# Fewer row maxima behind mid-product visits, a fixed score tile, another bank and a longer wait for blocks in a fused attention and MLP kernel

## The chip, the cores and the metric

The kernel runs on one core of one Trainium2 chip. The core has a matrix engine (PE, with its weight loads listed apart as PEld), a vector engine (DVE), a scalar engine (ACT), GpSimd (POOL), a sync engine (SP) that issues most transfers, and 16 DMA engines. Matrix products land in PSUM, whose banks hold 128 x 512 float32 values each; DVE and ACT read them from there. The metric is the device time of one execution in microseconds (us); lower is better.

## The reference

One transformer block with conditioning: a layer norm with scale and shift, softmax attention with 16 heads of width 28 over 2048 tokens of width 448, a gated residual, a second layer norm with scale and shift, an MLP of width 1792, and a second gated residual.

```python
mod = (_silu(c) @ w_mod).reshape(c.shape[0], 6, 1, -1)
sa, ca, ga, sb, cb, gb = (mod[:, 0], ..., mod[:, 5])
h = _layernorm(x, axis=-1) * (1 + ca) + sa
x = x + ga * _A_ref(h, A_wqkv, A_wo)      # softmax(q k^T / sqrt(28)) v, then wo
h = _layernorm(x, axis=-1) * (1 + cb) + sb
x = x + gb * _B_ref(h, B_w1, B_b1, B_w2, B_b2)   # layernorm, w1, gelu, w2
```

Softmax is taken with the maximum of each row subtracted. The maximum has to be known before the exponentials, so the kernel computes rough scores a second time for the maxima alone.

## The kernel before

Heads are taken in four groups `g` of four heads `j`. The 28 rows of head `j` lie on partitions 32`j` to 32`j`+27, so a product over 28 rows uses one of four row groups of the matrix engine. Queries come in four blocks `qt` of 512; a **unit** `u = 4g + qt` is one group and one block of queries. Keys come in four blocks `cch` of 512, or in 16 tiles `kt` of 128.

**A row maximum** (`max_one`, L478) is one product of 128 queries with 512 keys of one head into one PSUM bank (`max_mm`, L476) and a DVE reduction of that bank (L481). A full problem has 1024 of them. Some are taken in pairs: `pair_diff` (L485) and `open_pair` (L630) multiply with the difference of two key blocks, let ACT take the positive part (L489, L641), and a second product with one DVE operation (L493, L648) adds it and reduces. A pair costs two products and one DVE operation in place of two. Differences of key blocks are made on POOL by `make_kd` (L603). The banks for maxima go round in `mx_ring` (`ps_mx`): `ma`, `ma`, `m2`, `m2`, `m1` in the projection stage, later `m1`, `m2`, `m2` or `m1` alone. When a bank's turn comes, the product waits until DVE or ACT has read it.

**The projection stage** (to about 170 us) goes block by block of 512 tokens, `b` = 0 to 3, through a list of tasks `n`: chains of 11 products for q, k (`qk_task`, L396 by way of `mm_acc`) and v (`v_task`). After each chain `emit_task` (L687) puts a few maxima, four for `b` = 0 and five after it, one more where `sixth` holds: first the difference products, then single maxima with the second products of the pairs set in at place two. For the tasks (1,1), (1,3), (1,5), (1,7) and (2,8), `emit_mid` (L715) puts up to four more maxima between the halves of the chain. These are the mid-product visits. The tasks (1,0) to (1,3) end with products for the modulation rows (`mod_mm`, L747).

**The attention stage** (about 170 to 818 us) has 256 steps, 16 for each unit. A step computes two score tiles of 128 keys by 1024 (two heads each, three products for the split of float32 into a high and a low part: 12 products, L1297), lets ACT take exponentials of each tile (L1310, two for a step) and puts the products with v of the step before (L1255) behind them. Maxima are set in between. Up to step 118 a step works with two score tiles `s1`, `s0` and three or four maxima (`open_pair` on odd steps). From step `RING` = 119 on there is a ring of three score tiles: `third_tile` takes the two `m2` banks for `s2`, the first score tile is `s0`, the second `s1` or `s2` in turn, and the third of them serves for one wide pair of maxima (`emit_pair`, one DVE reduction of 1024 values, L684); a single maximum uses `m1`. That is three maxima a step. In steps 8 to 11 of the last four units (`is_wo`) the ring is left: `t_wo` (L1030) puts chains for the output projection into a bank of `mx_ring`, ACT copies the result (L1044), and `m2` serves maxima again. When all maxima are done, `three` is set and the ring goes on with score tiles alone.

Blocks of queries and keys of the next group are loaded by `load_hi` (L508) when the blocks before them are done with; `loaded` notes the step from which they may be used, three steps on. `emit_single` and `emit_pair` choose among `ready_max()`. `max_fin` and its `put` (L528) write a unit's negated maxima into its query tile some steps before the unit begins.

**The MLP stage** (to the end) runs chains of 11 products (L396) and three products for each token tile (L1376 to L1378) back to back.

Of the kernel before, what the change touches and what calls it, by code (L numbers as in the profile page):

```python
# [33 lines left out]
LAST_MAX = NKT - 4  # L34
RING = 119
PAIR_AT = (2, 2, 0, 2)
# [8 lines left out]
def tile_adaln_block(ctx: ExitStack, tc: tile.TileContext, x, wqkv, wo, w1, b1, w2, b2, c, w_mod, out):  # L45
# [22 lines left out]
    mx_ring = ["ma", "ma", "m2", "m2", "m1"]  # L68
# [39 lines left out]
    def ps_mx():  # L108
        mx_ring.append(mx_ring.pop(0))
        return ps_tile(mx_ring[-1], 1 if mx_ring[-1] == "m1" else 2)  # L110
# [392 lines left out]
    def load_hi(kind, g, b):  # L503
        loaded[(kind, g, b)] = clock[0] + 3
        tg = ("kh" if kind else "qh") + str(b)
        t = sb.tile([128, 512], F32R, tag=tg, name=nm(tg), bufs=1)
        (kh_sb if kind else qh_sb)[(g, b)] = t
        sp.dma_start(f(t), f(dscr[kind][0][g])[:, b * 512 : (b + 1) * 512])  # L508
        if kind and b in (PAIR_AT[g], PAIR_AT[g] + 1) and all((g, PAIR_AT[g] + c) in kh_sb for c in range(2)):
            at(clock[0] + 4, lambda: make_kd(g))  # L510
# [91 lines left out]

    def make_kd(g):  # L603
        if g and any(m[0] == kd["g"] for m in pairable()):
            at(clock[0] + 2, lambda: make_kd(g))
            return
        c0 = PAIR_AT[g]
        kd.update(g=g, t=slot("d0h", [128, 1, 512]), **{"from": clock[0] + 1})
        pool.tensor_tensor(out=kd["t"][:, 0, :], in0=f(kh_sb[(g, c0 + 1)]), in1=f(kh_sb[(g, c0)]), op=ALU.subtract)
# [81 lines left out]
    def emit_task(n, sixth, n_pairs):  # L691
# [4 lines left out]
        js = [m[3] for m in pairs]  # L696
        n_ops = n - len(pairs) + (sixth and len(pairs) > 0)
        singles = []
        for x in range(n_ops - len(pairs)):
            if mxq:  # L700

                free = [j for j in range(4) if j not in js] or range(4)
                fits = [y for y, m in enumerate(mxq[:16]) if m[:3] == mxq[0][:3] and m[4] == free[x % len(free)]]
                singles.append(mxq.pop(fits[0] if fits else 0))
        ops = [lambda ps, m=m: max_one(*m, ps) for m in singles]
        ops[2:2] = rests
        for x, op in enumerate(ops):
# [7 lines left out]
    def emit_mid():  # L715
        for j in range(4):
            fits = [x for x, m in enumerate(mxq[:16]) if m[4] == j]
            if fits:
                m = mxq.pop(fits[0])
                max_one(*m)  # L720
                count(*m[:2], [m[2]])

    p1_n = [0, False, 1, None]

# [88 lines left out]
    for b in range(NB):  # L813
# [12 lines left out]
        for n, (tb, kind, g) in enumerate(tasks):  # L826
# [11 lines left out]
            p1_n[2] = (3 if n > 4 else 1) if b == 3 else 2 if b == 2 and p1_n[1] else 1  # L838
            p1_n[3] = emit_mid if (b, n) in ((1, 1), (1, 3), (1, 5), (1, 7), (2, 8)) else None
            if kind < 2:  # L840
                fn = qk_task(tb, kind, g, firsts[n] if b == 0 and n < 3 else None)
# [70 lines left out]
    for key in ("s0", "s1"):  # L912
        ps_open(key)
    turns = ("s1", "s2")

# [73 lines left out]
    def unit_end_tasks(u, o_sb):  # L989
# [40 lines left out]
        def t_wo(t):  # L1030
            def go():
                p = ps_mx()
                ts = slice(t * 128, (t + 1) * 128)
# [229 lines left out]
    for u in range(NU):  # L1263
        g, qt = divmod(u, NB)
        for kt in range(NKT):
# [7 lines left out]
            if not (three or mxq or late):  # L1273
                three = True
                s_ring[:] = ["s0", turns[step % 2], turns[1 - step % 2]]
            now[0] = turns[step % 2]
# [13 lines left out]
            for n, hf in enumerate((first, 1 - first)):  # L1290
                s2 = ps_s2() if three else ps_two((now[0] if n else "s0") if ring else ("s1", "s0")[n if step < RING else 1 - n])
                for term, (kp, qp) in enumerate(((0, 0), (1, 0), (0, 1))):
# [149 lines left out]
```

## Time and profile before

| | |
|---|---|
| median of 3 runs | 1115.26 us (1115.2 to 1115.96) |
| profiled execution, its own time | 1116.36 us |
| its span, first to last instruction | 1114.3 us |
| PE busy | 1101.0 us, 99% of the span |
| DVE, ACT, POOL busy | 806.9, 693.2, 214.7 us |
| granted PE clock | 1.000 |

Views of the profile are read as follows. A row of the timeline has the start in us from the begin of the span, the length in us, the engine and line of the kernel, the operation with output<-inputs (buffer numbers left out: `m` is a bank of maxima, `s` a score tile, `pa` a chain's bank), partitions x elements, and the count of merged instructions; in brackets stands the idle time before it and what ended it. Products on PE overlap: one takes about 0.4 to 0.5 us from start to end, while the next may start after 0.2 us, or at once on another row group. So the busy share of PE hides small stalls, and the distance from start to start is what has to be read. A row of stretches gives, for a stretch of the span, its length, the busy time of each engine with the count of instructions, the granted clock, the share of the DMA engines and their GB/s.

### The profile page before, as it was taken

Reading aid. Unit: us, or ns where it says so; the run is one execution under the profiler, and the core shown is the slowest. Engines: PE = TensorE matmul, PEld = TensorE weight load, DVE = VectorE, ACT = ScalarE, POOL = GpSimd, SP = SyncE. Lnnn points to the kernel's source line nnn. Section 1 sums busy time; section 2 is a strip of 40 time slices with the busy share of each in tenths; the row PEclk is TensorE's granted clock in tenths of the full one; section 3 lists DMA queues with packets and bytes.
Section 4 is the critical chain, followed back from the end, with each engine's and each line's share of the span. In section 5 each row is a group of like instructions: output and inputs, shape, how many; then the busy total and the mean of one; then the engine's idle time right before and its main releaser. Section 6 shows DMA issues by size and latency. Waiting matters only on the chain.

```text
span 1114.3 us, 20698 instructions
## 1 busy us (share of the span) xinstructions
PE 1101.0 (99%) x8319; PEld 667.1 (60%) x8319; DVE 806.9 (72%) x1392; ACT 693.2 (62%) x878; POOL 214.7 (19%) x215
## 2 busy tenths in 40 slices
PE   8999999999999999999999999999999999999998
PEld 5756675444444444444444454544568888888887
DVE  6969788999999999988888867584558844444322
ACT  4555667888888888888888878577752311111210
POOL 1633332110000000000100020206214514023000
PEclk9999999999999999999999999999999999999999
DMA  9553354221231211221211402112222100000000
GB/s 307 204 187 97 100 179 129 58 68 30 77 96 51 68 41 46 67 90 58 69 40 59 125 30 87 58 30 75 75 81 67 31 34 1 1 34 1 34 1 34
DMA packets 49341, 81.19 MB, mean 73 GB/s; under 512 B 12311, under 2 KB 18702, under 8 KB 49234
## 3 DMA queue, kind: packets, MB, share of 16 engines
q1 hardware_dynamic: 48762, 79.14, 22.8%
q8 instruction: 65, 1.06, 0.4%
q10 hardware_dynamic: 148, 0.46, 0.1%
q0 software_dynamic: 336, 0.28, 0.1%
q14 instruction: 30, 0.25, 0.1%
HBM read 55.04 MB, written 26.48 MB: 73 GB/s over the span
## 4 chain that ended last, share of the span: by engine, by line
PE 93%; DVE 3%; ACT 1%; DMA 1%; issue 1%; SPq 0%; POOL 0%; DVEq 0%; ACTq 0%; POOLq 0%
PE s L1297 22%; PE o L1255 22%; PE m L396 16%; PE pa L396 9%; PE m L476 8%; PE s L1377 3%; PE s L1376 3%; PE s L1378 3%; PE s L476 1%; DVE mxp L481 1%; PE t L1377 1%; PE t L1378 1%; PE t L1376 1%; PE ma L476 1%; DMA slot_c<-in_w_mod_dram 1%
## 5 line engine op out<-in xcount | busy, mean ns | idle before, releaser
L481 DVE TENSOR_REDUCE mxp<-m 128x1 f32<-128x512 f32 x564 | 366.0, 686 | 82.9 <-PE m L476 66.4
L1297 PE MATMUL s<-slot_b,slot_a 28*128 28x512 f32 (+1 forms) x3072 | 358.1, 424 | 0.5 <-ACT slot_c0h L1310 0.5
L1297 PEld LDWEIGHTS s<-slot_b,slot_a 28*128 28x128 f32 (+1 forms) x3072 | 211.2, 183 | 170.7 <-ACT slot_c L1310 93.1
L476 PE MATMUL m<-kh,qh 28*128 28x512 f32 x598 | 221.6, 470 | 1.8 <-DMA kh<-d 1.0
L1310 ACT ACTIVATE slot_c<-s 128x1024 f32<-128x1024 f32 x170 | 174.7, 1027 | 53.5 <-PE s L1297 52.7
L1255 PE MATMUL o<-slot_c,v 128*32 128x512 f32 x680 | 178.9, 605 | 0.0
L1353 ACT ACTIVATE full<-m,b_col 128x512 f32<-128x512 f32 x56 | 38.5, 688 | 191.9 <-PE m L396 179.7
L1255 PE MATMUL o<-slot_c1h,v 128*32 128x512 f32 x512 | 134.7, 605 | 0.9 <-ACT slot_c1h L1310 0.9
L1255 PE MATMUL o<-slot_c0h,v 128*32 128x512 f32 x512 | 134.7, 605 | 0.0
L1310 ACT ACTIVATE slot_c0h<-s 128x1024 f32<-128x1024 f32 x128 | 131.5, 1027 | 2.5 <-PE m L396 2.5
L684 DVE TENSOR_REDUCE mxp<-s 128x2 f32<-128x1024 f32 x105 | 128.7, 1225 | 4.2 <-PE s L476 0.2
L1310 ACT ACTIVATE slot_c1h<-s 128x1024 f32<-128x1024 f32 x128 | 130.8, 1022 | 0.0
L1356 DVE CAST hi<-full 128x512 fp32r<-128x512 f32 x56 | 25.2, 450 | 134.7 <-ACT full L1353 134.7
L1310 ACT ACTIVATE slot_d<-s 128x1024 f32<-128x1024 f32 x86 | 88.3, 1027 | 27.7 <-PE s L1297 27.3
L476 PEld LDWEIGHTS m<-kh,qh 28*128 28x128 f32 x598 | 89.0, 182 | 18.0 <-DVE mxp L481 12.5
L1013 POOL TENSOR_TENSOR osb<-osb,osb 128x512 f32<-128x512 f32 x16 | 20.9, 1306 | 369.3 <-DMA osb<-drec 304.2
L1255 PE MATMUL o<-slot_d,v 128*32 128x512 f32 x344 | 90.5, 605 | 0.4 <-ACT osb L1219 0.4
L396 PE MATMUL m<-y,slot_a 128*128 128x512 f32 x160 | 60.7, 395 | 0.0
L648 DVE CUSTOM_DVE_ANT_0 slot_d0i<-m,slot_d0i 128x512 f32<-128x512 f32 x55 | 38.0, 691 | 14.5 <-PE m L476 10.8
L1357 DVE TENSOR_TENSOR lo<-full,hi 128x512 fp32r<-128x512 f32 x56 | 44.2, 789 | 5.6 <-DVE hi L1356 0.5
L1255 PEld LDWEIGHTS o<-slot_c,v 128*32 128x32 f32 x680 | 24.5, 108 | 39.4 <-issue 37.2
L476 PE MATMUL s<-kh,qh 28*128 28x512 f32 x210 | 46.2, 435 | 0.0
(341 smaller groups left out, 1841.8 us busy)
## 6 DMA issues: line engine op xcount, KB each, us to landing
slot_b<-d SPq DMA_DIRECT2D x32, 256.0 KB
slot_a<-d SPq DMA_DIRECT2D x32, 256.0 KB
d<-lo SPq DMA_DIRECT2D x28, 256.0 KB
d<-hi SPq DMA_DIRECT2D x16, 256.0 KB
osb<-drec SPq DMA_DIRECT2D x15, 256.0 KB
out_dram<-xn SPq DMA_DIRECT2D x16, 224.0 KB
raw<-in_B_w_dram SPq DMA_DIRECT2D x14, 224.0 KB
qh<-d SPq DMA_DIRECT2D x12, 256.0 KB
```

The costliest lines, as they stand in the source:

```text
L396: pe.matmul(p, a, b, start=(i == 0), stop=(i == len(terms) - 1))
L476: pe.matmul(m, qh_sb[(g, qt)][js, i * 128 : (i + 1) * 128], k[js, :], start=True, stop=True)
L481: dve.tensor_reduce(out=mxp[(g, qt)][:, i, j, cch : cch + 1], in_=m, op=ALU.max, axis=AX.X)
L684: dve.tensor_reduce(out=mxp[(g, qt)][:, i, j : j + 2, cch], in_=t, op=ALU.max, axis=AX.X)
L1255: pe.matmul(o[32 * j : 32 * j + 32, :], v_sb[kt // 4][:, kt % 4, 4 * g + j, :], p[j // 2][:, j % 2, :], start=(kt == 0), stop=(kt == NKT - 1),
L1297: pe.matmul(s2[:, jj, :], ks[rows_, kp, kc], qs[rows_, qp, :], start=(term == 0), stop=(term == 2))
L1310: act.activation(pt[hf], s2, AF.Exp, scale=SCALE)
L1353: act.activation(gf, p, AF.Gelu_apprx_tanh, bias=b1_col[:, i : i + 1])
L1357: dve.tensor_tensor(out=glo, in0=gf, in1=f(ghi), op=ALU.subtract)
L1376: pe.matmul(pp, ghi[:, ts], w_hi, start=(m == 0), stop=False)
L1377: pe.matmul(pp, ghi[:, ts], w_lo, start=False, stop=False)
L1378: pe.matmul(pp, glo[:, ts], w_hi, start=False, stop=(m == NFT - 1))
```

## The change

Four things are changed, and with them the order in which maxima are chosen:

- In the five tasks with a mid-product visit, `emit_task` gets one maximum fewer (`p1_n[0] -= ...`). `emit_task` chooses singles by row group among the first 24 of the queue (in block 3 only of the same unit's), and the second products of pairs come at place `4 - len(pairs)` instead of two.
- The first score tile of the ring is `s1` where it was `s0`, and the second is `s0` or `s2`; steps without the ring use `s1`, `s0` throughout. `RING` is 121 instead of 119.
- The last of the four projection chains of a unit (`t == 3`) passes over `m1` where other banks are in the ring.
- A block loaded from step `RING` on may be used five steps after its load instead of three, and `make_kd` does nothing from step `RING` on.

```diff
-RING = 119
+RING = 121
...
     def load_hi(kind, g, b):
-        loaded[(kind, g, b)] = clock[0] + 3
+        loaded[(kind, g, b)] = clock[0] + (5 if clock[0] >= RING else 3)
...
     def make_kd(g):
+        if clock[0] >= RING:
+            return
         if g and any(m[0] == kd["g"] for m in pairable()):
...
         n_ops = n - len(pairs) + (sixth and len(pairs) > 0)
+        free = [j for j in range(4) if j not in js]
         singles = []
         for x in range(n_ops - len(pairs)):
             if mxq:
-
-                free = [j for j in range(4) if j not in js] or range(4)
-                fits = [y for y, m in enumerate(mxq[:16]) if m[:3] == mxq[0][:3] and m[4] == free[x % len(free)]]
-                singles.append(mxq.pop(fits[0] if fits else 0))
+                near = [m for m in mxq[:24] if not p1_n[4] or m[:2] == mxq[0][:2]]
+                want = free[x % len(free)] if free else x % 4
+                singles.append(min(near, key=lambda m: m[4] != want))
+                mxq.remove(singles[-1])
         ops = [lambda ps, m=m: max_one(*m, ps) for m in singles]
-        ops[2:2] = rests
+        first = max(0, 4 - len(pairs))
+        ops[first:first] = rests
...
     def emit_mid():
         for j in range(4):
-            fits = [x for x, m in enumerate(mxq[:16]) if m[4] == j]
+            fits = [x for x, m in enumerate(mxq[:24]) if m[4] == j]
...
             p1_n[3] = emit_mid if (b, n) in ((1, 1), (1, 3), (1, 5), (1, 7), (2, 8)) else None
+            p1_n[4] = not more
+            p1_n[0] -= p1_n[3] is not None
...
-    turns = ("s1", "s2")
+    turns = ("s0", "s2")
...
         def t_wo(t):
             def go():
+                if t == 3 and mx_ring[0] == "m1" and len(mx_ring) > 1:
+                    mx_ring.append(mx_ring.pop(0))
                 p = ps_mx()
...
-                s_ring[:] = ["s0", turns[step % 2], turns[1 - step % 2]]
+                s_ring[:] = ["s1", turns[step % 2], turns[1 - step % 2]]
...
-                s2 = ps_s2() if three else ps_two((now[0] if n else "s0") if ring else ("s1", "s0")[n if step < RING else 1 - n])
+                s2 = ps_s2() if three else ps_two(now[0] if ring and n else ("s1", "s0")[n])
```

The number of products stays 7258 instructions of PE in the program; DVE has two operations more, ACT one fewer, POOL one fewer. The order of the instructions shows where they went. On PE, the second half of task (1,1)'s chain and the maxima behind it stood like this before (`kh`, `qh`, `raw`: blocks of keys, queries, and the key difference; the name before the arrow is the bank):

```order
L396 MATMUL pa_173_773<-slot_c0h_111_510,slot_a2h_21_126 128x512
L476 MATMUL ma_179_799<-raw_165_734,qh1_158_707 128x512
L476 MATMUL m2_180_802<-kh1_162_729,qh0_60_322 128x512
L476 MATMUL m2_181_805<-kh1_162_729,qh0_60_322 128x512
L476 MATMUL m1_182_808<-kh0_74_360,qh1_158_707 128x512
L476 MATMUL ma_183_811<-kh1_162_729,qh0_60_322 128x512
L747 MATMUL o_171_760<-slot_v3_117_524,slot_d0_4_86 32x448 x4
```

and stand like this now:

```order
L396 MATMUL pa_173_773<-slot_c0h_111_510,slot_a2h_21_126 128x512
L476 MATMUL ma_179_799<-raw_165_734,qh1_158_707 128x512
L476 MATMUL m2_180_802<-kh1_162_729,qh0_60_322 128x512
L476 MATMUL m2_181_805<-kh1_162_729,qh0_60_322 128x512
L476 MATMUL m1_182_808<-kh0_74_360,qh1_158_707 128x512
L751 MATMUL o_171_760<-slot_v3_117_524,slot_d0_4_86 32x448 x4
```

The fifth maximum is gone; the four before it stand in the same banks. The entry into the ring on PE, from the second score tile of the last step without it to the first of the ring (`o` is the products with v), was before:

```order
L1297 MATMUL s0_1605_6458<-slot_b1_1416_5708,slot_a1_1093_4449 128x512 x6
L476 MATMUL m1_1606_6465<-kh2_1239_5013,qh2_1087_4420 128x512
L476 MATMUL m2_1607_6468<-kh3_1240_5015,qh2_1087_4420 128x512
L1255 MATMUL o_1552_6253<-slot_d0_1593_6411,v1_230 32x512 x2
L1255 MATMUL o_1552_6253<-slot_c1h_1594_6412,v1_230 32x512 x2
L1297 MATMUL s0_1610_6482<-slot_b1_1416_5708,slot_a1_1093_4449 128x512 x2
```

and is now, two steps later:

```order
L1305 MATMUL s0_1614_6507<-slot_b1_1405_5680,slot_a2_976_3992 128x512 x6
L476 MATMUL m1_1615_6514<-kh3_1234_4998,qh2_1092_4443 128x512
L476 MATMUL m2_1616_6517<-kh3_1234_4998,qh2_1092_4443 128x512
L1263 MATMUL o_1541_6225<-slot_c1_1601_6457,v1_230 32x512 x2
L1263 MATMUL o_1541_6225<-slot_c1h_1602_6458,v1_230 32x512 x2
L1305 MATMUL s1_1619_6531<-slot_b1_1405_5680,slot_a2_976_3992 128x512 x2
```

The next score tile is now `s1`, not the `s0` just written. The end of the last projection chain of unit 12 and the start of step 204 behind it on PE (`slot_e`: the output weights) were before:

```order
L396 MATMUL m1_2199_9192<-slot_e1_492_2043,hi_2163_9021 128x448
L396 MATMUL m1_2199_9192<-slot_e0_491_2042,lo_2164_9022 128x448
L1297 MATMUL s0_2203_9211<-slot_b0_2010_8319,slot_a3_2106_8763 128x512 x2
L476 MATMUL m1_2204_9214<-kh3_1826_7463,qh2_1690_6842 128x512
L1297 MATMUL s0_2203_9211<-slot_b0_2010_8319,slot_a3_2106_8763 128x512 x4
```

and are now:

```order
L396 MATMUL m2_2194_9178<-slot_e1_487_2028,hi_2158_9007 128x448
L396 MATMUL m2_2194_9178<-slot_e0_486_2027,lo_2159_9008 128x448
L1305 MATMUL s1_2198_9197<-slot_b0_2005_8305,slot_a3_2101_8749 128x512 x2
L476 MATMUL m1_2199_9200<-kh3_1834_7509,qh2_1698_6888 128x512
L1305 MATMUL s1_2198_9197<-slot_b0_2005_8305,slot_a3_2101_8749 128x512 x4
```

The chain lies in `m2` and the maximum behind it in `m1`. Further, as the order has it: the projection stage holds 204 products for maxima instead of 209; steps 0 to 127 hold 499 in both; step 233 has three instead of one and step 234 three instead of none; all other ring steps hold three in both. Steps 79 and 81 lose the first product of a pair, step 117 gains one. Block 2 of the keys of group 3 is loaded in step 151 and first used in step 157 (before: loaded in step 149, used in 152). Block 1 of the keys of group 2 is loaded in step 78 and first used in 81 (before: 72 and 78), with blocks 2 and 3 and a block of queries loaded in step 79 as before.

2 lines of the change are left out of this document (1 added, 1 removed).

## The prediction

> **What bounds the kernel now.** I read the page first, then the timeline of PE around each place that the change touches, then stretches by stage. PE is the bound: it is 99% busy, and it carries the chain that ended last:
>
> ```profile
> PE 93%; DVE 3%; ACT 1%; DMA 1%; issue 1%; SPq 0%; POOL 0%; DVEq 0%; ACTq 0%; POOLq 0%
> PE s L1297 22%; PE o L1255 22%; PE m L396 16%; PE pa L396 9%; PE m L476 8%; PE s L1377 3%; PE s L1376 3%; PE s L1378 3%; PE s L476 1%; DVE mxp L481 1%; PE t L1377 1%; PE t L1378 1%; PE t L1376 1%; PE ma L476 1%; DMA slot_c<-in_w_mod_dram 1%
> ```
>
> The program has as many PE instructions after the change as before. So a gain can only be a stall of PE that goes, or products that move to where they run beside others. The 3% on DVE is where to look: PE waits for a bank that DVE has still to reduce. The stalls are small, and I look for them one by one in the distances from start to start.
>
> **Maxima in the projection stage.** First a visit without a wait. Five maxima behind a chain need two rounds, since two of them share a row group:
>
> ```profile
> 67.28 0.49 PE L476 MATMUL ma<-raw,qh 28*128 28x512 f32 x1
> ...
> 67.94 0.96 PE L747 MATMUL o<-slot_v,slot_d 128*32 128x448 f32 x8
> ```
>
> That is 0.66 us from the first maximum to the next work. In task (1,1), four maxima stand in the middle of the chain, and the five behind it look like this:
>
> ```profile
> 62.20 0.50 PE L476 MATMUL ma<-raw,qh 28*128 28x512 f32 x1
> 62.20 0.93 PE L476 MATMUL m<-kh,qh 28*128 28x512 f32 x3
> 63.24 0.50 PE L476 MATMUL ma<-kh,qh 28*128 28x512 f32 x1
> 63.67 0.96 PE L747 MATMUL o<-slot_v,slot_d 128*32 128x448 f32 x8
> ```
>
> The visit takes 1.47 us. The row of three ends at 63.13; its last product, as long as its neighbours (0.5), started near 62.64, and the fifth 0.60 later. That is the pace at which DVE frees banks, not that of PE. The change takes the fifth away. What follows then comes 0.43 behind the fourth (as 63.67 stands behind 63.24), at 63.07: a gain of 0.60. Tasks (1,3) and (1,5) have the same shape of banks, and I take the same for each. In (1,7) and (2,8) it is otherwise:
>
> ```profile
> 91.24 0.49 PE L476 MATMUL ma<-kh,qh 28*128 28x512 f32 x1 [0.33 <-DVE mxp L481]
> 91.59 0.49 PE L476 MATMUL m<-raw,osb 28*128 28x512 f32 x1
> 92.01 0.33 PE L277 MATMUL o<-ident,xn 128*128 128x128 f32 x1
> ...
> 134.89 0.49 PE L476 MATMUL ma<-raw,osb 28*128 28x512 f32 x1
> 135.49 0.49 PE L476 MATMUL ma<-kh,qh 28*128 28x512 f32 x1
> 135.49 0.49 PE L476 MATMUL o<-kh,qh 28*128 28x512 f32 x1
> ```
>
> In (1,7) the fifth comes only 0.35 behind the fourth; the gain is 0.35. In (2,8) the sixth started together with the fifth, in the bank `o`; taking it away gains nothing. Together 3 x 0.60 + 0.35 = 2.15 us. It could be nothing where DVE, not the visit, sets the pace over several tasks, and 3.0 (five times 0.60) if (1,7) and (2,8) gain fully too.
>
> The new choice of row groups spares a third round in places such as this visit, where six maxima stood in groups 2, 3, 1, 2, 2, 3 and now stand in 2, 3, 0, 1, 2, 3:
>
> ```profile
> 142.05 0.50 PE L476 MATMUL m<-raw,qh 28*128 28x512 f32 x2
> ...
> 142.94 0.50 PE L396 MATMUL pa<-slot_c,slot_a 128*128 128x512 f32 x1
> ```
>
> That took 0.89 against 0.66 for two rounds: 0.23 us. Other visits of six that run over two rounds could give as much again, or nothing where the wait is for a bank. I take 0.3 in all, between 0 and 1.0. So the stage ends about 2.45 us earlier. What hides this edit's other side is the transfer of the modulation weights (for L747), needed 0.6 us earlier than now; if it is not there, up to that 0.6 comes back.
>
> **Blocks five steps behind their load.** The chain that ended last has one transfer in the ring, and PE stands still for it:
>
> ```profile
> 540.03 5.74 DMA kh<-d
> ```
>
> ```profile
> 543.84 0.60 PE L1255 MATMUL o<-slot_c0h,v 128*32 128x512 f32 x2
> 544.37 0.50 PE L1297 MATMUL s<-slot_b,slot_a 29*128 29x512 f32 x2
> 545.90 0.46 PE L476 MATMUL m<-kh,qh 28*128 28x512 f32 x1 [1.03 <-DMA kh<-d]
> ```
>
> The maximum and the score products behind it come 1.53 us after the start of the step. In a step without a wait the next products come 0.34 after it:
>
> ```profile
> 666.75 0.49 PE L1297 MATMUL s<-slot_b,slot_a 29*128 29x512 f32 x2
> ...
> 667.09 0.63 PE L1297 MATMUL s<-slot_b,slot_a 28*128 28x512 f32 x8
> ...
> 667.88 0.62 PE L1255 MATMUL o<-slot_c,v 128*32 128x512 f32 x2
> ```
>
> So the stall is 1.19 us. Now this block is used six steps after its load. How long a step is, the exponentials tell (two for a step; the rows are of their line alone, first the steps without the ring, then the ring):
>
> ```profile
> 200.00:450.00 250.00, 194.26 (x200) 1.00 0.19 59
> 560.00:650.00 90.00, 77.69 (x81) 1.00 0.25 75
> ```
>
> 250 us for 100 steps is 2.50 us, 90 us for 40.5 steps 2.22. Six ring steps are 13.3 us against the 5.74 of the transfer, so all of 1.19 goes: -1.2. It is zero only if another load stalls in its place. The three maxima of each step stay in the order, so none is starved by the longer wait. The Trainium skill, DMA: Bandwidth & Descriptors, section Measured (HBM→SBUF, 128 partitions, SWDGE, issued from GpSimd), has 0.95 us for 64 KB and 6.15 for 1 MB; by an estimate between them these 256 KB would take some 2.3 us, three steps would suffice, and this part would be worth 0. The trace does not agree: this transfer was issued among others and took 5.74.
>
> **The last projection chain on another bank.** Behind the chains of units 12 and 13 the first maximum of the next step stands in `m1`, which ACT has still to copy:
>
> ```profile
> 670.89 0.50 PE L1297 MATMUL s<-slot_b,slot_a 29*128 29x512 f32 x2
> 671.64 0.49 PE L476 MATMUL m<-kh,qh 28*128 28x512 f32 x1 [0.24 <-ACT full L1044]
> ...
> 719.07 0.50 PE L476 MATMUL m<-kh,qh 28*128 28x512 f32 x1 [0.24 <-ACT full L1044]
> ```
>
> 0.75 against 0.34 makes 0.41, twice: -0.8. The copy now holds `m2`, which becomes `s2`. The first product into `s2` stands behind ten score products of that step. In the step at 666.75 two of them start at once and eight more over a row of 0.63 us from 667.09, so it comes some 0.8 us into the step. The copy was done 0.75 into it (671.64): just covered. Without that cover up to 0.4 twice would come back.
>
> **Ring two steps later, `s1` fixed.** At the entry the ring's first tile is `s0`, which ACT still reads:
>
> ```profile
> 469.40 0.60 PE L1255 MATMUL o<-slot_c1h,v 128*32 128x512 f32 x2
> 470.19 0.50 PE L1297 MATMUL s<-slot_b,slot_a 29*128 29x512 f32 x2 [0.19 <-ACT slot_c0h L1310]
> ```
>
> 0.79 from row to row against 0.53 (543.84 to 544.37): 0.26 us go when the first tile is `s1`. In the ring itself `s0` and `s1` only change names. Two steps are now done without the ring, 2 x (2.50 - 2.22) = +0.56. Together +0.3, between -0.3 and +0.6.
>
> **Five maxima more at the end.** Steps 233 and 234 get two and three more. Of the steps with projections, one with three maxima took 1.13 us from its first score products to those with v (666.75 to 667.88), and one without any:
>
> ```profile
> 756.17 0.99 PE L1297 MATMUL s<-slot_b,slot_a 29*128 29x512 f32 x12
> 757.09 0.62 PE L1255 MATMUL o<-slot_c,v 128*32 128x512 f32 x2
> ```
>
> took 0.92. So step 234 costs +0.21, and step 233, which had one already, between 0 and +0.21: +0.3 in all. One POOL difference and the diff products that move in steps 79, 81 and 117 I leave at nothing, within 0.3 either way.
>
> **Sum.** -2.45 - 1.2 - 0.8 + 0.3 + 0.3 = -3.85 us. The profiled execution took 1116.36 (a span of 1114.3 and 2.06 around it), which makes 1112.5; the median of the runs, 1115.26, stands 1.1 below that execution, so I predict **1111.4 us**.
>
> **Rivals.**
>
> - *DVE sets the pace of the projection stage.* If its backlog lasts from task to task, a maximum less saves only where the stall shows, and the start of the next visit takes it back: the 2.45 shrink to some 0.5, 1113.4 us. For it: PE waits for DVE in exactly these visits. Against: the visit at 67.28, next to one that stalls, has no wait at all. 12%.
> - *The opposite.* Visits after a stalled one also start with banks held; with DVE freed of five reductions and row groups spread, up to 1.6 us more comes off (the upper bounds above: 3.0 + 1.0 - 2.45), 1109.8. For it: 142.05 is not the only long visit. Against: only one of its kind is taken apart here. 20%.
> - *The wait moves.* The longer wait for blocks does not do what it says, since other transfers of the ring take its place: 1112.6. Against: 13.3 us of room. 7%. The same time would come out by the figure of the Trainium skill, DMA: Bandwidth & Descriptors, named above, since three steps would then have sufficed.
> - *Slower.* Four loads for group 2 (three key blocks, one of queries) now fall into steps 78 and 79, and block 1 is used in step 81, three steps of 2.50 = 7.5 us after its issue. PE waits for it as in step 152. To make the kernel slower than before, the stall must eat 3.85: the block would land 11.4 us after its issue. Where three of them are issued now, the DMA engines are full for one stretch of 2 us only:
>
> ```profile
> 372.00:374.00 2.00, 2.00 (x25) 1.31 (x25) 1.96 (x5) 1.98 (x3) 0.00 (x0) 1.00 0.96 276
> ```
>
> That leaves room for a fourth. At 14 us, 6.5 of stall, the time would be 1117.9. 5%.
>
> **How the numbers follow.** The forecast has 56%. A difference of 0.2% or 2.2 us is about what can be told from no change, so "faster" ends at 1113.0. The forecast's own range is 1110.0 to 1112.9; with the opposite below and the first rival above, the range is **1108.6 to 1113.6**. Faster: 56 + 20 + 7 and a few of the first rival's, 0.84; within 0.2%: 0.11; slower: 0.05.
>
> **What would show it.** In the changed profile the first steps of the attention stage should stand some 2.4 us earlier. No visit behind a mid-product one should take over 1.3 us except (2,8). There should be no "DMA kh<-d" on the chain that ended last, no idle time behind "ACT full L1044" on a maximum's row in steps 204 and 220 (line 1052 now), and no 0.79 at the entry. The prediction is wrong if the projection stage is not shorter, or if a stall on a block shows up near step 81 or 152.

## The result and the profile after

The changed kernel takes 1111.77 us (median of 9 runs, 1111.07 to 1112.53); the kernel before took 1116.42 in the 9 runs beside them (1115.2 to 1117.88). The ratio is 0.9959, 95% interval 0.9948 to 0.9969: faster by 0.4%. A second set of 5 runs of the changed kernel gave 1111.95 and 0.9962 (0.9949 to 0.9974). The profiled execution, of the first set, took 1112.02 us, with a span of 1110.0. Both pages count 8319 instructions on PE, so PE has no less to do than before.

The chain that ended last, on the page of the changed kernel, answers to the one shown ahead of the prediction. DVE has gone from 3% to 2% and PE from 93% to 95%; the chain is still PE's:

```profile
PE 95%; DVE 2%; ACT 1%; issue 1%; DMA 1%; SPq 0%; POOL 0%; DVEq 0%; ACTq 0%; POOLq 0%
PE s L1305 23%; PE o L1263 23%; PE m L396 16%; PE pa L396 9%; PE m L476 8%; PE s L1385 3%; PE s L1386 3%; PE s L1384 3%; PE s L476 2%; PE t L1385 1%; PE t L1386 1%; PE t L1384 1%; PE o L277 1%; DMA slot_c<-in_w_mod_dram 1%; DVE mxp L481 1%
```

To see where the time went, the start of a step is taken as the start of its first exponential on ACT, and the projection stage begins with the first product of L396. The columns are lengths in us in the two profiled executions:

| stretch | before | after | difference |
|---|---|---|---|
| first chain to step 0 (projection stage) | 145.70 | 143.39 | -2.31 |
| steps 0 to 117 | 295.88 | 295.92 | +0.04 |
| 117 to 123 (entry into the ring) | 14.02 | 14.50 | +0.48 |
| 123 to 150 | 60.73 | 60.81 | +0.08 |
| 150 to 153 (wait for a block) | 8.22 | 6.71 | -1.51 |
| 153 to 203 | 118.76 | 118.84 | +0.08 |
| 203 to 205 (behind unit 12's last chain) | 7.01 | 6.35 | -0.66 |
| 205 to 219 | 39.80 | 39.92 | +0.12 |
| 219 to 221 (behind unit 13's last chain) | 7.65 | 6.96 | -0.69 |
| 221 to 231 | 22.46 | 22.51 | +0.05 |
| 231 to 236 (five maxima more) | 21.59 | 21.88 | +0.29 |
| 236 to the end | 348.03 | 348.06 | +0.03 |
| sum | | | -4.00 |

The spans differ by 4.35; the other 0.35 lies ahead of the first chain. It is no part of the change: the same changed kernel, profiled twice, began its first chain at 24.1 and at 25.2 us, as the rows of L396 in the stretch up to 31 us have it (after the colon the ns of one instruction, then the first and the last start). First the changed kernel:

```profile
L396 PE MATMUL pa<-slot_b,slot_a x20: 388/394/499, 24.1 to 30.6; 128*128 128x512 f32 x20
```

and its second profile:

```profile
L396 PE MATMUL pa<-slot_b,slot_a x17: 392/394/503, 25.2 to 30.8; 128*128 128x512 f32 x17
```

So all differences below are taken behind that start. The PE timeline of the changed kernel shows the visits. From the first maximum to the next work, the visits of (1,1), (1,7) and (2,8), and the one that stood at 142.05 before:

```profile
61.85 0.50 PE L476 MATMUL ma<-raw,qh 28*128 28x512 f32 x1
...
62.72 0.96 PE L751 MATMUL o<-slot_v,slot_d 128*32 128x448 f32 x8
...
88.33 0.50 PE L476 MATMUL ma<-raw,qh 28*128 28x512 f32 x1
...
89.16 0.50 PE L476 MATMUL m<-kh,qh 28*128 28x512 f32 x1 [0.32 <-DVE mxp L481]
89.58 0.66 PE L277 MATMUL o<-ident,xn 128*128 128x128 f32 x4
...
131.91 0.50 PE L476 MATMUL m<-raw,qh 28*128 28x512 f32 x2
...
133.09 0.50 PE L476 MATMUL m<-kh,qh 28*128 28x512 f32 x1
133.52 1.19 PE L396 MATMUL pa<-slot_c,slot_a 128*128 128x512 f32 x4
...
139.61 0.50 PE L476 MATMUL m<-raw,qh 28*128 28x512 f32 x2
...
140.27 1.20 PE L396 MATMUL pa<-slot_c,slot_a 128*128 128x512 f32 x4
```

(1,1) takes 0.87 where it took 1.47; (1,3) and (1,5), read in the same way, 0.87 and 0.98 for 1.50 and 1.59. (1,7) takes 1.25 for 1.60 and still waits for DVE. (2,8) takes 1.61 for 1.58, so it gained nothing: the one maximum less is a product that had stood beside another. The visit of six takes 0.66 for 0.89.

Next, the same timeline where PE stood still for a block, at the entry into the ring, and behind unit 12's last chain:

```profile
471.90 0.60 PE L1263 MATMUL o<-slot_c,v 128*32 128x512 f32 x2
...
472.44 0.49 PE L1305 MATMUL s<-slot_b,slot_a 29*128 29x512 f32 x2
...
544.42 0.50 PE L1305 MATMUL s<-slot_b,slot_a 29*128 29x512 f32 x2
544.43 0.50 PE L476 MATMUL m<-kh,qh 28*128 28x512 f32 x1
544.76 0.83 PE L1305 MATMUL s<-slot_b,slot_a 28*128 28x512 f32 x8
...
667.44 0.49 PE L476 MATMUL m<-kh,qh 28*128 28x512 f32 x1
...
668.62 0.62 PE L1263 MATMUL o<-slot_c,v 128*32 128x512 f32 x2
```

The entry takes 0.54 from row to row (0.79 before). The step at 544.42 starts its maximum beside its first score products, with no idle time ahead of it. In step 204 the first maximum starts with the scores instead of 0.75 behind them, and the products with v come 1.18 after it. In the kernel before, 1.88 passed between the two, from the scores at 670.89 to this row of its PE timeline:

```profile
672.77 0.62 PE L1255 MATMUL o<-slot_c,v 128*32 128x512 f32 x2
```

### The profile page after: what moved, and what is told of

It is laid out like the page before. It is cut to its first block, busy times and chain, and to the rows that moved or that the text cites. A ratio compares the mean times of both kernels' runs of the same rounds, so it can differ in the third digit from the quotient of the medians.

```text
span 1110.0 us, 20703 instructions
## 1 busy us (share of the span) xinstructions
PE 1098.9 (99%) x8319; PEld 665.7 (60%) x8319; DVE 807.2 (73%) x1394; ACT 693.0 (62%) x877; POOL 213.9 (19%) x214
## 4 chain that ended last, share of the span: by engine, by line
PE 95%; DVE 2%; ACT 1%; issue 1%; DMA 1%; SPq 0%; POOL 0%; DVEq 0%; ACTq 0%; POOLq 0%
PE s L1305 23%; PE o L1263 23%; PE m L396 16%; PE pa L396 9%; PE m L476 8%; PE s L1385 3%; PE s L1386 3%; PE s L1384 3%; PE s L476 2%; PE t L1385 1%; PE t L1386 1%; PE t L1384 1%; PE o L277 1%; DMA slot_c<-in_w_mod_dram 1%; DVE mxp L481 1%
## 5 line engine op out<-in xcount | busy, mean ns | idle before, releaser
L476 PE MATMUL m<-kh,qh 28*128 28x512 f32 x615 | 229.3, 468 | 0.6 <-DVE mxp L481 0.3
L686 DVE TENSOR_REDUCE mxp<-s 128x2 f32<-128x1024 f32 x103 | 126.2, 1226 | 5.1
L476 PEld LDWEIGHTS m<-kh,qh 28*128 28x128 f32 x615 | 92.0, 182 | 16.6 <-DVE mxp L481 13.1
L396 PE MATMUL m<-y,slot_a 128*128 128x512 f32 x160 | 60.6, 395 | 0.0
L481 DVE TENSOR_REDUCE mxp<-ma 128x1 f32<-128x512 f32 x61 | 39.5, 681 | 13.3 <-PE m L476 8.9
```

The lines of the kernel that those rows point to most:

```text
L396: pe.matmul(p, a, b, start=(i == 0), stop=(i == len(terms) - 1))
L476: pe.matmul(m, qh_sb[(g, qt)][js, i * 128 : (i + 1) * 128], k[js, :], start=True, stop=True)
L481: dve.tensor_reduce(out=mxp[(g, qt)][:, i, j, cch : cch + 1], in_=m, op=ALU.max, axis=AX.X)
L686: dve.tensor_reduce(out=mxp[(g, qt)][:, i, j : j + 2, cch], in_=t, op=ALU.max, axis=AX.X)
```

## The experiments

Each edit is made to the changed kernel, and the difference quoted is against its profile, but for u8_rec, which edits the kernel before. Differences are taken over the stretches of the table above, behind the start of the first chain. Five profiles differ in nothing up to step 117 (the changed kernel twice, u2_bank, u3_load, u6_s0); they put the projection stage at 143.23 to 143.40 us, and the steps 0 to 117 at 295.92 to 296.09. So a difference of 0.2 in a long stretch, or in a sum, says little. Short stretches whose order is the same agree within 0.1. In the names, u stands for one thing undone or moved, x for a further step.

**The maximum fewer undone (u1_mid).**

```diff
-            p1_n[0] -= p1_n[3] is not None
```

> The changed kernel with the fifth maximum behind the mid-product visits put back (the tasks (1,1), (1,3), (1,5), (1,7), (2,8) take as many maxima as before). Theory (PE waits there for the bank that DVE frees): the visits of (1,1), (1,3), (1,5) go from about 0.87-0.98 us back to 1.47-1.59, (1,7) from 1.25 to 1.60, (2,8) stays within 0.1; the projection stage is 2.1 us longer, and with five maxima fewer at its end the attention stage is about 0.3 us shorter: span near 1111.8. Rival (DVE's backlog sets the pace over several tasks, so the visit's gain is taken back later): the visits change but the stage's end moves by less than 1 us.

Measured: 1113.73 us in one run. The projection stage is 2.09 longer; the five visits take 1.47, 1.49, 1.59, 1.62 and 1.62. Steps 231 to 236 are 0.50 shorter, all else together +0.08; sum +1.67. The visit of (1,1) on the PE timeline is that of the kernel before again:

```profile
62.08 0.94 PE L476 MATMUL m<-kh,qh 28*128 28x512 f32 x3
63.12 0.50 PE L476 MATMUL ma<-kh,qh 28*128 28x512 f32 x1
63.55 0.96 PE L751 MATMUL o<-slot_v,slot_d 128*32 128x448 f32 x8
```

So the gain of the stage is the five visits' own. The visits beside them stayed at 0.66, so DVE does not set the pace of the whole stage; that rival has fallen. A detail matters below: with this order of maxima the block at step 149 is loaded right behind a broadcast again, is used in step 155, and nothing waits for it.

**The bank undone (u2_bank).**

```diff
-                if t == 3 and mx_ring[0] == "m1" and len(mx_ring) > 1:
-                    mx_ring.append(mx_ring.pop(0))
```

> The changed kernel without the rule that passes over m1 for the fourth projection chain. Theory: steps 204 and 220 wait again for ACT's copy, 0.41 us each by the distance to the first maximum, 0.6 each when the whole of the two steps behind the chain is counted (that is what the two traces differ by there): span 1110.8 to 1111.2, everything up to step 203 unchanged. Rival (the changed order of maxima, not the bank, shortened these steps): no change at steps 204 and 220, span 1110.0.

Measured: 1113.75 us in one run; +0.70 in steps 203 to 205, +0.71 in 219 to 221, and no other stretch by more than 0.17. Sum +1.32. The PE timeline in step 204:

```profile
667.98 0.50 PE L1303 MATMUL s<-slot_b,slot_a 29*128 29x512 f32 x2
668.73 0.49 PE L476 MATMUL m<-kh,qh 28*128 28x512 f32 x1 [0.24 <-ACT full L1050]
668.73 0.74 PE L1303 MATMUL s<-slot_b,slot_a 28*128 28x512 f32 x7
...
669.85 0.62 PE L1261 MATMUL o<-slot_c,v 128*32 128x512 f32 x2
```

From the first scores to the products with v it takes 1.87, against 1.18 in the changed kernel: 0.69. The prediction had 0.41, the delay of the row at 668.73 alone (0.75 against 0.34). The rest, 0.28, comes behind that row: from it to the products with v it takes 1.12, where 1.18 less the 0.34 of a step without a wait leaves 0.84. I read it so: without a wait the maximum runs beside the first two score products, on another row group, and costs PE nothing of its own; held back by ACT, it needs a place among the others. The cover that the prediction feared for holds: in the changed kernel, where the chain lies in `m2`, no product of steps 204 and 220 stands behind idle time of PE that ACT's copy ended.

**Three steps for a block again (u3_load).**

```diff
-        loaded[(kind, g, b)] = clock[0] + (5 if clock[0] >= RING else 3)
+        loaded[(kind, g, b)] = clock[0] + 3
```

> The changed kernel with three steps instead of five between a ring load and its first use; the block loaded in step 151 is used in 154 instead of 157. Theory (the transfer lands some 6 us after its issue and three ring steps of 2.22 us are too few beside the other work): a stall near 1.2 us in step 154, span about 1111.2. Rival (the stall came from what was issued together with the load in the kernel before, and is gone with the other order): no stall over 0.3 us in step 154, span 1110.0.

Measured: 1112.47 us in one run, sum +0.17, and no stall: steps 150 to 153 and 153 to 157 differ by under 0.03. The theory that the two steps more had taken the stall fell, since the block is now used in step 154, three steps after its load, and PE does not wait for it:

```profile
547.28 0.50 PE L1305 MATMUL s<-slot_b,slot_a 29*128 29x512 f32 x2
547.29 0.50 PE L476 MATMUL m<-kh,qh 28*128 28x512 f32 x1
```

By the last update of its semaphore in the trace the block, issued at 541.80, landed at 544.77, 2.97 us later. In the kernel before, the same block was issued at 540.03 and landed at 545.77, 5.74 later. Where the difference comes from, SP's queue shows (a row with x2 holds two loads, and the first is the block in question). The kernel before:

```profile
539.43 0.56 SPq L1008 DMA_DIRECT2D osb<-drec  x1
540.03 0.95 SPq L508 DMA_DIRECT2D kh<-d  x2
```

and the changed kernel:

```profile
537.34 0.55 SPq L1014 DMA_DIRECT2D osb<-drec  x1
541.25 1.79 SPq L508 DMA_DIRECT2D kh<-d  x2
```

`osb<-drec` spreads a unit's reciprocals over the partitions, 256 KB like the block. Before, the block was issued 0.60 us behind it, now 3.91. The stretches of the two profiles over 542 to 544 us (after the clock, the share of the DMA engines and their GB/s) show the crowd, first before:

```profile
542.00:544.00 2.00, 2.00 (x27) 1.07 (x23) 1.80 (x3) 1.66 (x3) 0.00 (x0) 1.00 0.98 265
```

and after:

```profile
542.00:544.00 2.00, 2.00 (x27) 0.99 (x23) 1.72 (x4) 1.78 (x3) 1.28 (x1) 1.00 0.64 156
```

The load has moved because the order of maxima has: its old block is done with in step 151 now, not 149.

**Maximum and three steps undone together (u7_mid_load).** This brings the load back to step 149 and leaves it three steps.

```diff
-        loaded[(kind, g, b)] = clock[0] + (5 if clock[0] >= RING else 3)
+        loaded[(kind, g, b)] = clock[0] + 3
...
-            p1_n[0] -= p1_n[3] is not None
```

> The changed kernel with the fifth maxima back (as in the run u1_mid, where the block is loaded in step 149 just behind the broadcast of the reciprocals and lands 5.6 us later) and with three steps instead of five, so that the block is used in step 152 as in the kernel before. Theory (the stall needs a load that lands late because other transfers run beside it; only then do five steps help): a stall of 1.0 to 1.4 us in step 152, which u1_mid does not have; everything else as in u1_mid. Rival (the stall is gone for another reason): none over 0.3.

Measured: 1115.2 us in one run; the projection stage +2.02, steps 150 to 153 +1.52, steps 231 to 236 -0.51; sum +3.01. The stall is back, on the PE timeline:

```profile
544.93 0.50 PE L1304 MATMUL s<-slot_b,slot_a 29*128 29x512 f32 x2
546.47 0.46 PE L476 MATMUL m<-kh,qh 28*128 28x512 f32 x1 [1.03 <-DMA kh<-d]
```

and the cause in SP's queue, the load 0.60 us behind the broadcast:

```profile
539.99 0.56 SPq L1013 DMA_DIRECT2D osb<-drec  x1
540.59 0.95 SPq L508 DMA_DIRECT2D kh<-d  x2
```

It landed 5.75 us after its issue. Together these kernels make a square:

| | load 0.6 us behind the broadcast | load some 3.9 us behind it |
|---|---|---|
| used three steps later | stall (u7_mid_load, the kernel before) | none (u3_load) |
| used six steps later | none (u1_mid) | none (the changed kernel) |

Either of the two, the longer wait or the later load, takes the stall. The change does both, and the second came as a side effect of the other maxima. It is easily lost: in u4_ring119, u5_groups and x3_late2 (below) the block is loaded 0.6 us behind the broadcast again and lands 5.13 to 5.22 us after its issue, and with the longer wait PE does not stand still for it (steps 150 to 153 differ by no more than 0.01).

**Reciprocals spread three steps later, in the kernel before (u8_rec).** The other way to part the two transfers.

```diff
-        times = (0, 3, 9, 10) if staged else (0, 1, 5, 6)
+        times = (0, 6, 9, 10) if staged else (0, 1, 5, 6)
```

> The kernel before, with the reciprocals' broadcast of each unit whose output is staged three steps later (in step 151 instead of 148 for the unit in question), so that it is no longer issued 0.6 us ahead of the block's load. Theory (the broadcast stretches the landing from about 3.0 to 5.7 us): the block lands within 4.4 us and the stall of 1.2 us in step 152 is gone or under 0.4; span about 1113.2. Rival (three steps are too few whatever runs beside the load): the stall stays at 1.0 or more.

Measured: 1116.58 us in one run, against 1116.93 for the kernel before on the same chip. The load is now issued at 539.00, ahead of the broadcast, and landed at 541.89, 2.9 us later; the stall at step 152 is gone (-1.48 in steps 150 to 153). But +1.44 appear between steps 188 and 190, and the span is 1114.7, not the 1113.2 expected. The broadcast of a later unit, at 620.36 in place of 614.21, is now what is late. POOL, DVE and PE in the timeline there:

```profile
625.63 1.28 POOL L1013 TENSOR_TENSOR osb<-osb,osb 128x512 f32<-128x512 f32 x1 [34.03 <-DMA osb<-drec]
626.94 0.43 DVE L1023 CAST hi<-osb 128x512 fp32r<-128x512 f32 x1 [1.39 <-POOL osb L1013]
...
628.02 0.49 PE L476 MATMUL m<-kh,qh 28*128 28x512 f32 x1
...
629.43 0.49 PE L1297 MATMUL s<-slot_b,slot_a 29*128 29x512 f32 x2 [0.67 <-DVE mxp L684]
```

The cast waits on DVE 1.39 us for POOL's product, which waits for the broadcast. The reductions of the banks stand behind the cast in DVE's queue, and PE waits for one of them. The cast and the split stayed at their step while their input came three steps later: a stall was moved from one transfer to another.

**The ring at 119 (u4_ring119).**

```diff
-RING = 121
+RING = 119
```

> The changed kernel with the ring from step 119 as before. Theory (a step without the ring costs 2.50 us and one with it 2.22, and s1 as first tile takes the stall at the entry away by itself): 0.5 us shorter between steps 117 and 123, given back in part by three maxima in step 235 (0.2): span 1109.7, and the entry shows 0.53 us, not 0.79, between the last products with v and the first score products. Rival (the two later steps are what removes the stall): 0.79 again at the entry and span 1110.3 or more.

Measured: 1112.13 us in one run; steps 117 to 123 -0.55, steps 231 to 236 +0.61, the rest -0.21; sum -0.15. The two steps in the ring are worth 0.55, as 2 x (2.50 - 2.22) had it. But a step without the ring holds up to four maxima, and one of the ring three; what no longer fits stands at the end, in step 235 too, and costs as much. A single run can't tell -0.15 from nothing. Without the later ring the entry does not stall either, 0.53 from row to row, so that part is `s1`'s alone.

**`s0` first in the ring again (u6_s0).**

```diff
-    turns = ("s0", "s2")
+    turns = ("s1", "s2")
...
-                s_ring[:] = ["s1", turns[step % 2], turns[1 - step % 2]]
+                s_ring[:] = ["s0", turns[step % 2], turns[1 - step % 2]]
...
-                s2 = ps_s2() if three else ps_two(now[0] if ring and n else ("s1", "s0")[n])
+                s2 = ps_s2() if three else ps_two((now[0] if n else "s0") if ring else ("s1", "s0")[n if step < RING else 1 - n])
```

> The changed kernel with s0 as the ring's first tile, as before, entry still at step 121. Theory: the first score products of step 121 wait for ACT's exponentials of s0, 0.79 us instead of 0.53 behind the last products with v, and nothing else moves: 0.2 to 0.35 us. Rival (the entry is as fast with s0, since step 120 is other than step 118): no difference over 0.1.

Measured: 1113.12 us in one run, of which 0.95 lie ahead of the first chain; behind it the sum is +0.16. The entry on the PE timeline waits for ACT again, 0.78 from row to row:

```profile
472.94 0.60 PE L1263 MATMUL o<-slot_c1h,v 128*32 128x512 f32 x2
473.72 0.50 PE L1305 MATMUL s<-slot_b,slot_a 29*128 29x512 f32 x2 [0.18 <-ACT slot_c0h L1318]
```

Steps 117 to 123 are 0.17 longer and 123 to 128 0.15 shorter. The stall at the entry is real, but the next steps give most of it back: the fixed `s1` is worth about nothing.

**The old choice and place of row groups (u5_groups).**

```diff
-                near = [m for m in mxq[:24] if not p1_n[4] or m[:2] == mxq[0][:2]]
-                want = free[x % len(free)] if free else x % 4
-                singles.append(min(near, key=lambda m: m[4] != want))
-                mxq.remove(singles[-1])
+                free = [j for j in range(4) if j not in js] or range(4)
+                fits = [y for y, m in enumerate(mxq[:16]) if m[:3] == mxq[0][:3] and m[4] == free[x % len(free)]]
+                singles.append(mxq.pop(fits[0] if fits else 0))
...
-        first = max(0, 4 - len(pairs))
-        ops[first:first] = rests
+        ops[2:2] = rests
```

> The changed kernel with the old choice of singles by row group and the old place of the pairs' second products. Theory (a third round costs 0.23 us, and only where one is spared): the projection stage is 0.2 to 0.4 us longer, its visits of six in block 3 show up to 0.89 us again; span 1110.2 to 1110.5. Rival (row groups spread over the whole stage free DVE and PE everywhere): over 1 us longer.

Measured: 1112.66 us in one run. The projection stage is 0.23 longer, and one visit takes a third round, 0.89 for 0.66, on the PE timeline:

```profile
75.98 0.49 PE L476 MATMUL m<-raw,qh 28*128 28x512 f32 x1
...
76.55 0.39 PE L476 MATMUL ma<-kh,qh 28*128 28x512 f32 x1
76.87 0.33 PE L277 MATMUL o<-ident,xn 128*128 128x128 f32 x1
```

The visits of block 3 are as long with the old choice as in the changed kernel, so the visit at 142.05 was not cured by this rule alone. Steps 79 to 83 are 0.31 longer, 203 to 205 0.29, others shorter; sum +0.53. The size of the prediction's 0.3 is about right, its place is not fixed: which visit stumbles changes with the order of the whole queue.

**Further: two maxima fewer (x1_two), the same with the ring at 119 (x2_two119), and the changed kernel beside them (after_again).** If each visit is as long as DVE keeps the banks, a second maximum less should pay again.

```diff
-            p1_n[0] -= p1_n[3] is not None
+            p1_n[0] -= 2 * (p1_n[3] is not None)
```

> The changed kernel, unaltered, beside the kernel before in five rounds, as the measure for the next two runs. Both theories: 4.0 to 4.6 us below the kernel before, as in the runs shown (1116.42 and 1111.77 at the median).

> Two maxima fewer, instead of one, at the five visits behind a mid-product one. Theory (each visit is as long as DVE needs for the banks that are still held, so a further maximum less shortens it again): the visits of tasks (1,1), (1,3) and (1,5) fall from 0.87, 0.87 and 0.98 to about 0.45, that of (1,7) from 1.25 to about 0.65, that of (2,8) from 1.61 to between 1.0 and 1.6; 1.9 to 3.1 us less in the projection stage. Five more maxima then stand in the attention stage, at up to 0.1 us each, and some steps get four (0.1 each): +0.5 to +0.9. Sum against the changed kernel: -1.0 to -2.6 us. Rival (DVE is behind over the whole stage, so the next visits take back what these give): the visits named become shorter, but their neighbours longer; the stage gains under 0.6 us and the kernel is as long as the changed one or up to 0.6 longer.

> As the run with two maxima fewer, and the ring two steps earlier (119 instead of 121). Theory (two steps by the ring's 2.22 instead of 2.50 us gain 0.56, the maxima that the ring can't hold cost about as much at the end, as one look at the ring alone showed: -0.15 in all): within 0.4 us of the run with two maxima fewer. Rival (the ring's start is worth its 0.56 us alone): 0.5 us or more below it.

Measured, at the median: after_again 1111.95, x1_two 1112.93, x2_two119 1113.72, with ratios to the kernel before of 0.9962 (0.9949 to 0.9974), 0.9968 (0.9956 to 0.9981) and 0.9975 (0.9965 to 0.9984). In x1_two the projection stage came at -1.98, the low end of what was expected, with visits of 0.66, 0.66, 0.65, 0.66 and 1.00. The first three were expected at 0.45. Their last product starts 0.34 behind the first, with no idle time ahead of it: it is the second product of a pair, on the row group of the pair's first. So what is left there is a second round and no wait for DVE. The price was mis-sized. The three steps from each ring step with a fourth maximum (150, 179, 211) cost 0.90, 0.88 and 0.70, where some 0.1 for each such step was expected, and steps 231 to 236 cost 0.62; the sum is +1.17. The PE timeline at step 150 shows why:

```profile
537.16 0.50 PE L476 MATMUL m<-kh,qh 28*128 28x512 f32 x1
537.59 0.62 PE L1263 MATMUL o<-slot_c1h,v 128*32 128x512 f32 x2
...
538.58 0.95 PE L1305 MATMUL s<-slot_b,slot_a 29*128 29x512 f32 x7
539.16 0.49 PE L476 MATMUL m<-kh,qh 28*128 28x512 f32 x1
```

and its DVE row for the bank in question:

```profile
538.42 0.68 DVE L481 TENSOR_REDUCE mxp<-m 128x1 f32<-128x512 f32 x1
```

The fourth product stands by itself for 0.43. DVE reduces its bank only at 538.42, behind a wide pair, and the next step's maximum, which needs the same bank, comes at 539.16, 0.58 behind the scores of its step instead of beside them. As in u2_bank, a maximum comes late because its bank is still to be read, here by DVE. In x2_two119 five ring steps have a fourth maximum (138, 157, 175, 195, 221); the three steps from each cost 0.72 to 0.88. Neither expectation for it holds.

**Two fewer only where no fourth one follows (x3_late2).**

```diff
-            p1_n[0] -= p1_n[3] is not None
+            p1_n[0] -= (p1_n[3] is not None) * (1 + ((b, n) in ((1, 7), (2, 8))))
```

> Two maxima fewer only at the visits of tasks (1,7) and (2,8), one fewer at the other three, so that two maxima instead of five move into the attention stage and no ring step gets a fourth. Theory (the run with two fewer everywhere lost its gain to three ring steps with four maxima, 0.7 to 0.9 us each, and to its last steps): these two visits fall from 1.25 and 1.61 to 0.66 and 1.00 as they did there, 1.2 us; no step between 123 and 221 costs over 0.2 more than in the changed kernel; steps 231 to 236 cost +0.4 to +0.7. Sum: 0.5 to 0.8 us below the changed kernel, some 1111.3. Rival (every maximum moved into the ring costs about 0.3 wherever it stands, and the rest of the loss was that): the stage between steps 123 and 221 is 0.6 us or more longer, and the kernel is as long as the changed one.

Measured: 1112.53 us at the median of 6 runs; the ratio is 0.9957 (0.9944 to 0.9969), which can't be told from the changed kernel's. The visits came as expected, 0.66 for (1,7) and 0.97 for (2,8), on the PE timeline:

```profile
88.86 0.49 PE L476 MATMUL ma<-raw,qh 28*128 28x512 f32 x1
...
89.52 0.66 PE L277 MATMUL o<-ident,xn 128*128 128x128 f32 x4
...
131.84 0.50 PE L476 MATMUL m<-raw,qh 28*128 28x512 f32 x2
...
132.81 1.19 PE L396 MATMUL pa<-slot_c,slot_a 128*128 128x512 f32 x4
```

The stage gains 1.28. Steps 123 to 221 together cost 0.08, so the maxima in the ring are not the price here, and the rival falls there. But 231 to 236 cost 0.63, 64 to 79 0.28 and 117 to 123 0.24, and the sum is +0.06. The last two were in no expectation; what in the order of maxima makes them was not taken apart. No version of these beats the changed kernel.

## Why the prediction was right, and where not

The forecast was 1111.4 us and -3.85; the medians gave 1111.77 and -4.65, and the trace -4.00 behind the first chain. That the time came within 0.4 us is in part luck. The forecast started from 1115.26, the median of three runs, while the nine runs of the kernel before have 1116.42; from there its -3.85 would have made 1112.57. What makes the 0.65 between medians and trace was not taken apart; the start of the first chain varies by more. By its terms:

| term | predicted | measured | from |
|---|---|---|---|
| five mid-product visits | -2.15 | -2.16 | visits, u1_mid |
| row groups | -0.3 | -0.15 | rest of the stage (u5_groups: 0.23) |
| stall on a block | -1.2 | -1.51, then +0.14 | steps 150 to 157 |
| last chain on another bank | -0.8 | -1.35, then +0.12 and +0.05 | steps 203 to 221, u2_bank |
| ring later, `s1` fixed | +0.3 | +0.48 | steps 117 to 123 |
| five maxima at the end | +0.3 | +0.29 | steps 231 to 236 |

- **The visits** were right one by one: 0.60 (three times 0.60 to 0.63 measured), 0.35 for (1,7) and nothing for (2,8). The pace was DVE's, and the visits, not the stage, were what waited. The 0.15 left for the row groups is within what two profiles of this stage differ by; one visit took a third round less, 0.66 for 0.89. The modulation weights for L751 came early enough: the work at 62.72 has no idle time ahead of it.
- **The block** is where the prediction failed in its cause. The step was: "Now this block is used six steps after its load ... so all of 1.19 goes". The stall went, but u3_load shows that it goes at three steps as well, and the longer wait is worth 0 in the changed kernel: that this term came out is luck. The prediction read the 5.74 us as the duration of this transfer, when it was the duration of this transfer behind a broadcast 0.60 us ahead of it. The part on the change has the load in step 151 instead of 149, and the prediction did not ask what stands in SP's queue there. The longer wait is not useless: in u1_mid it alone takes the stall. The Trainium skill, DMA: Bandwidth & Descriptors, section Measured (HBM→SBUF, 128 partitions, SWDGE, issued from GpSimd), has 0.95 us for 64 KB and 6.15 for 1 MB; the prediction's estimate between them was 2.3 us for these 256 KB, by which three steps suffice, and it set that aside for the 5.74. The runs put a load with room at 2.9 to 3.2 from issue to landing, somewhat above that estimate, and the crowded one at 5.7, far from it.
- **The bank** was right in mechanism and mis-sized: 0.41 each was the delay of the late product; 0.66 to 0.71 was the price, since it also loses its place beside the scores.
- **The ring** term's parts were right apart (0.25 at the entry, 0.55 for two steps), but u6_s0 shows that the first is given back at once. And the two steps were counted apart from the five maxima, though they are one account: u4_ring119 gains the one and pays the other.
- **The rivals.** DVE's pace: no, the neighbours of the shortened visits kept 0.66. The opposite: no, the stage came 2.31 shorter and not more than the 2.45 forecast; (2,8) gained nothing, and one maximum more had to go to open it. The wait moves: no, no other load took the stall's place, and its going is worth 1.37 (steps 150 to 157). That three steps suffice, as that rival adds, is so only where the load does not stand behind the broadcast (u3_load against u7_mid_load). A new stall near step 81: no, steps 79 to 83 differ by under 0.05.

## What to carry to other kernels

A wait on a transfer in the chain says that the transfer was late, not how long such a transfer takes: look at what was issued just ahead of it in the same queue, and whether the change moves either of the two, before the wait itself is lengthened. A small product that is held back costs its delay and the place beside other products that it loses, so a stall is best measured to the next large group, not to the late row. Work taken out of a stalled place has to stand somewhere else: count the free places first, since one too many in a step cost here more than the stall that it left.

## What was not expected of the hardware

- A block of 256 KB landed 2.97 us after its issue (u3_load), 3.21 in the changed kernel (541.25 to 544.46) and 2.89 ahead of the broadcast (u8_rec), but 5.74 and 5.75 when it was issued 0.60 us behind the broadcast (the kernel before, u7_mid_load). In these two kernels another two loads follow within 1.0 us, and in the kernel before the DMA engines were then busy 0.98 of the time, at 265 GB/s. The loads that follow are the smaller part of it: in u4_ring119, u5_groups and x3_late2 the block stands 0.6 us behind the broadcast, nothing else is issued for the next 3.2 us, and it still lands 5.13 to 5.22 after its issue.
- The broadcast itself, 256 KB like the block, is slower than the block even with room: 5.11 us in the chain of waits of u8_rec (620.36), where SP issued nothing else in the 4 us behind it. In a stretch of that time, with nothing else under way, a quarter of the DMA engines is busy (share 0.24, at 94 GB/s), as the stretches of that profile have it:

```profile
622.00:624.00 2.00, 2.00 (x27) 0.95 (x23) 1.75 (x3) 1.78 (x3) 0.00 (x0) 1.00 0.24 94
```

So it runs on four of the 16. Its source is written as 4 rows of 32 copies (`broadcast_to([4, 32, 512])`). The Trainium skill, DMA: Bandwidth & Descriptors, section Rules for kernel authors, says that a transfer whose outermost dimension counts fewer than 16 stays on at most that many engines; this trace agrees, with the 0.24. It also fits how the block came in: in the kernel before, the last four updates of the broadcast's semaphore came between 544.42 and 545.18. Of the block's 16 updates 12 had come by 544.24, and the last four came between 545.15 and 545.77; in the changed kernel all 16 came within one us (543.49 to 544.46). By that reading four engines, busy with the broadcast, held up the whole block. Spreading the broadcast over 16 engines would be the next thing to try; it was not tried.
- The start of the first chain varied by 1.07 us between two executions of one kernel, as much as the smaller parts of this change are worth together; why was not looked into.
